# A recurrent two-layer kernel with streamed weights: half-size weight tiles, a deeper ring, later weight copies, and one-lane first and last steps

## The chip, the core and the metric

The kernel runs on one core of one Trainium2 chip. The metric is the device time of one execution in microseconds (us), the median of several. PE is the matrix engine, DVE the vector engine, ACT the scalar engine, POOL is GpSimd, SP the engine that here only issues DMAs. All timed runs of this study were in the fast state (mean granted PE clock of the profiled ones 0.981 to 0.992 of full speed).

## The reference

Two layers, A (attention with a memory that is carried from segment to segment) and B (dilated sliding-window attention), are applied twice: A, B, A, B.

```python
# A: S = 2048 tokens, Dm = 640, H = 32 heads of Dh = 192, segments of 32 tokens, memory of 8 tokens
mem = mem0
for s in range(64):
    h = concat([mem, x[32*s : 32*(s+1)]])         # 40 tokens
    q, k, v = h @ Wq, h @ Wk, h @ Wv              # 640 x 6144 each
    p = softmax(mask(q @ k.T * Dh**-0.5))
    o = (p @ v) @ Wo                              # 6144 x 640
    mem, out[s] = o[:8], o[8:]
# B: heads of 20, each token looks at itself and 7 tokens at distances 2, 4, ... 14
x = x + A(layernorm(x));  x = x + B(layernorm(x))
x = x + A(layernorm(x));  x = x + B(layernorm(x))
```

The memory makes the 64 segments sequential. Only part of the weights of A (31.5 MB) is kept on the chip; the rest is read again in every step.

## The kernel before

The second A, B pair runs three segments behind the first as a second *lane*: each step t handles segment t of the first pair and segment t - 3 of the second, 40 + 40 = 80 columns. So there are 67 steps. In the first three and the last three, one lane has nothing to do but is computed all the same. Eight groups of four heads make a step:

```python
def unit(self, kind, i):                       # one of 32 weight tiles of 983 KB
    ...
    if res: t_ = self.wres.tile([P, 3840], BF16, ...)          # 14 stay on the chip
    else:   t_ = self.wring.tile([P, 3840], BF16, name="w_ring")   # 18 pass through 4 slots
    if (kind, i) in self.wcopy:
        nc.sync.dma_start(out=t_[:], in_=self.wcopy[(kind, i)][:])    # rows of 7680 bytes
    else:
        nc.sync.dma_start(out=v, in_=src)                             # rows of 1536 or 1280 bytes
    ...
    elif (kind, i) not in self.wcopy:                                 # in step 0
        self.wcopy[(kind, i)] = self.dram.tile([P, 3840], BF16, ...)
        nc.gpsimd.dma_start(out=self.wcopy[(kind, i)][:], in_=t_[:])

def step(self, t):
    for i in range(NQUAD):                     # 8 groups
        self.a_k(i, t)                         # 30 matmuls of 80 columns, ACT copies the result
        self.a_q(i, t)                         # 30 of 80, DVE copies
        if i >= 2: self.a_o(i - 2)             # 30 of 80, into ps_acc
        if last: self.a_pv(i - 1); self.a_s(i)
        self.a_v(i, t)                         # 10 of 384
        if i >= 1 and not last: self.a_pv(i - 1)
        # ... here parts of layer B of the last two steps ...
        if not last: self.a_s(i)               # scores, 8 of 80
    # ... layer norm of the next segment, a_o(6), a_pv(7), B's projections, a_o(7), memory ...

def run(self, ctx):
    self.prologue()
    for t in range(self.n_seg + LAG + 2):      # the last two with layer B only
        self.step(t)
    self.y_store(yseg // 4)
```

The softmax here doesn't subtract the row's maximum and nothing guards it: scores larger than these inputs give would overflow.

Of the kernel before, what the change touches and what calls it, by code (L numbers as in the profile page):

```python
# [39 lines left out]
N_UNITS = 32  # L40
N_RES = 14
RING = 4


def unit_order():
    order = []
    for i in range(NQUAD):
        order.append(("k", i))
        order.append(("q", i))
        if i >= 2:  # L50
            order.append(("o", i - 2))
        order.append(("v", i))
    order += [("o", 6), ("o", 7)]
    return order


def resident_units():
    res = set()
    for n, u in enumerate(unit_order()):
        if (n * N_RES) // N_UNITS != ((n + 1) * N_RES) // N_UNITS:  # L60
            res.add(u)
    return res


class Kernel:
    def __init__(self, ctx, tc, A_x, A_mem0, A_Wq, A_Wk, A_Wv, A_Wo, B_wqkv, B_wo, out):
# [15 lines left out]
        self.ps_big = pool("ps_big", 4, space=PSUM)  # L82
# [4 lines left out]
        self.resident = resident_units()  # L87
        self.build_consts(B_wqkv, B_wo)

    def build_consts(self, B_wqkv, B_wo):  # L90
# [23 lines left out]

        def band(name, cur):
            m = cp.tile([P, NX], BF16, name=name)
            nc.gpsimd.memset(m[:], 0.0)
            for half in range(2):
                off = 0 if half == cur else SEG
                for l in range(2):  # L120
                    r0 = 64 * half + SEG * l
                    blk = m[r0:r0 + SEG, SEG * l:SEG * (l + 1)]
                    for w in range(BW):
                        nc.gpsimd.affine_select(out=blk, in_=blk, compare_op=ALU.not_equal, fill=1.0,
                                                base=off - BDIL * w, pattern=[[1, SEG]], channel_multiplier=-1)
            return m
# [19 lines left out]
        def pers(name, shape, n, dt=BF16, zero=True):  # L146
            ts = []
            for j in range(n):
                t_ = cp.tile(shape, dt, name=f"{name}{j}")
                if zero:  # L150
                    nc.vector.memset(t_[:], 0.0)
                ts.append(t_)
            return ts

        self.hT = pers("hT", [P, NC * NT + 88], 2)
        self.KF = pers("KF", [P, 4 * NT + 48], 2)
        self.Kz = pers("Kz", [P, 4 * NT + 48], 2)
        self.Vt = pers("Vt", [P, 1152], 2)
        self.xin = pers("xin", [P, NC, NX], 3)
        self.h2T = pers("h2T", [P, NC, P], 1)[0]  # L160
        self.KB = pers("KB", [P, NBC, P], 1)[0]
        self.VB = pers("VB", [P, BH // 2, 2 * BD + 1], 1)[0]
        nc.vector.memset(self.VB[:, :, BD:BD + 1], 1.0)
        self.On = pers("On", [P, 3 * P], 1)[0]
        self.YT = pers("YT", [P, NC, P], 1, zero=False)[0]
        self.m0T = pers("m0T", [P, NC, NM], 1, zero=False)[0]
        self.wqkv = cp.tile([P, NC, 3 * D], BF16, name="wqkv_sb")
        nc.scalar.dma_start(out=self.wqkv[:], in_=B_wqkv.rearrange("(c p) n -> p c n", p=P))
        self.wo = cp.tile([P, 2, 3, D], BF16, name="wo_sb")
        nc.vector.memset(self.wo[64:P, :, 2, :], 0.0)  # L170
        for par in range(2):
            r0 = par * (D // 2)
            nc.scalar.dma_start(out=self.wo[:, par, 0:2, :], in_=B_wo[r0:r0 + 2 * P, :].rearrange("(m p) n -> p m n", p=P))
            nc.scalar.dma_start(out=self.wo[0:64, par, 2, :], in_=B_wo[r0 + 2 * P:r0 + D // 2, :])

    def unit(self, kind, i):
        if (kind, i) in self.units:
            return self.units[(kind, i)]
        nc = self.nc
        res = (kind, i) in self.resident  # L180
        if kind == "o":
            src = self.wsrc["o"][QE * i:QE * (i + 1), :].rearrange("(m p) d -> p m d", p=P)
        else:
            src = self.wsrc[kind][:, QE * i:QE * (i + 1)].rearrange("(c p) n -> p c n", p=P)
        if res:
            t_ = self.wres.tile([P, 3840], BF16, name=f"w_{kind}{i}")
        else:
            t_ = self.wring.tile([P, 3840], BF16, name="w_ring")
        v = t_[:].rearrange("p (a b) -> p a b", a=6 if kind == "o" else NC)
        if (kind, i) in self.wcopy:  # L190
            nc.sync.dma_start(out=t_[:], in_=self.wcopy[(kind, i)][:])
        else:
            nc.sync.dma_start(out=v, in_=src)
        if res:
            self.units[(kind, i)] = v
        elif (kind, i) not in self.wcopy:
            self.wcopy[(kind, i)] = self.dram.tile([P, 3840], BF16, name=f"wc_{kind}{i}")
            nc.gpsimd.dma_start(out=self.wcopy[(kind, i)][:], in_=t_[:])
        return v
# [7 lines left out]
    def proj_stationary(self, kind, i, t):  # L207
        nc = self.nc
        w = self.unit(kind, i)
        hT = self.hT[t % 2]  # L210
        ps = self.big(f"ps_{kind}")
        for n in range(6):
            for c in range(NC):
                nc.tensor.matmul(ps[:, NT * n:NT * (n + 1)], lhsT=w[:, c, P * n:P * (n + 1)], rhs=hT[:, NT * c:NT * (c + 1)],  # L214
                                 start=(c == 0), stop=(c == NC - 1))
        return ps

    def a_k(self, i, t):
        nc = self.nc
        ps = self.proj_stationary("k", i, t)  # L220
        pv = ps[:, 0:6 * NT].rearrange("p (a b n) -> p a b n", a=2, b=3)
        h4 = lambda tl: tl[:, 0:4 * NT].rearrange("p (a j n) -> p a j n", a=2, j=2)
        kf, kz = h4(self.KF[i % 2]), h4(self.Kz[i % 2])
        nc.scalar.copy(out=kf, in_=pv[:, :, 0:3:2, :])  # L224
        nc.scalar.copy(out=kz[0:64, :, 0, :], in_=pv[0:64, :, 1, :])
        nc.scalar.copy(out=kz[64:P, :, 1, :], in_=pv[64:P, :, 1, :])

    def a_q(self, i, t):
        ps = self.proj_stationary("q", i, t)
        qt = self.ap2.tile([P, 6, NT], BF16, name="QT")  # L230
        self.nc.vector.tensor_copy(out=qt[:], in_=ps[:, 0:6 * NT].rearrange("p (a n) -> p a n", a=6))  # L231
        self.qt = qt

    def a_v(self, i, t):
        nc = self.nc
        w = self.unit("v", i)
        hT = self.hT[t % 2]
        vt = self.Vt[i % 2]
        for pr in range(2):
            ps = self.big("ps_v")  # L240
            for c in range(NC):
                nc.tensor.matmul(ps[:, 0:384], lhsT=hT[:, NT * c:NT * c + P], rhs=w[:, c, 384 * pr:384 * (pr + 1)],  # L242
                                 start=(c == 0), stop=(c == NC - 1))
            src = ps[0:NT, 0:384].rearrange("p (j e) -> p j e", j=2)
            dst = vt[0:NT, 512 * pr:512 * pr + 640].rearrange("p (j e) -> p j e", j=2)[:, :, 0:DH]
# [5 lines left out]
    def a_s(self, i):  # L251
        nc = self.nc
        ps = self.one("s")
        sv = ps[:, 0:4 * NT].rearrange("p (h n) -> p h n", h=4)
        kf, kz, qt = self.KF[i % 2], self.Kz[i % 2], self.qt
        for h in range(4):
            pr, j = h // 2, h % 2
            nc.tensor.matmul(sv[:, h, :], lhsT=kf[:, NT * h:NT * h + P], rhs=qt[:, 3 * pr + 2 * j, :], start=True, stop=False)  # L258
            nc.tensor.matmul(sv[:, h, :], lhsT=kz[:, NT * h:NT * h + P], rhs=qt[:, 3 * pr + 1, :], start=False, stop=True)  # L259
        e = self.ap2.tile([P, 4, NT], BF16, name="E")  # L260
        nc.scalar.activation(out=e[0:NT], in_=sv[0:NT], func=ACT.Exp, scale=float(DH) ** -0.5)  # L261
        em = self.ap2.tile([P, 4, NT], BF16, name="Em")
        nc.vector.tensor_tensor(out=em[0:NT], in0=e[0:NT], in1=self.maskA[0:NT, :].unsqueeze(1).to_broadcast([NT, 4, NT]), op=ALU.mult)
        self.em = em

    def a_pv(self, i):
        nc = self.nc
        em = self.em
        vt = self.Vt[i % 2]
        dn = self.one("d")  # L270
# [6 lines left out]
        r = self.ap2.tile([P, 2, 2, NT], F32, name="R")  # L277
# [9 lines left out]
    def a_o(self, i):  # L287
        nc = self.nc
        w = self.unit("o", i)
        ot = self.ots.pop(i)[:].rearrange("p a b n -> p (a b) n")  # L290
        if i == 0:
            self.acc = self.one("acc")
        for m in range(6):
            for c in range(NC):
                nc.tensor.matmul(self.acc[:, NT * c:NT * (c + 1)], lhsT=w[:, m, P * c:P * (c + 1)], rhs=ot[:, m, :],  # L295
# [5 lines left out]
    def mem_out(self, t):  # L301
        nc = self.nc
        a = self.lanes(self.acc[:, 0:NC * NT])
        h = self.lanes(self.hT[(t + 1) % 2][:, 0:NC * NT])
        if t + 1 == LAG:
            nc.vector.tensor_copy(out=h[:, :, 0, 0:NM], in_=a[:, :, 0, 0:NM])
            nc.vector.tensor_copy(out=h[:, :, 1, 0:NM], in_=self.m0T[:])
        else:
            nc.vector.tensor_copy(out=h[:, :, :, 0:NM], in_=a[:, :, :, 0:NM])

    def ln_sq(self, x):
        sq = self.bp.tile([P, NC, NX], BF16, name="sq")
# [11 lines left out]
    def ln_small(self, ps):  # L324
        nc = self.nc
        m = self.ap2.tile([P, NX], F32, name="ln_m")
# [3 lines left out]
        nc.vector.scalar_tensor_tensor(out=v[:], in0=ps[:, NX:2 * NX], scalar=1.0 / D, in1=v[:], op0=ALU.mult, op1=ALU.subtract)  # L330
        nc.scalar.activation(out=v[:], in_=v[:], func=ACT.Ln, bias=self.eps_t[:])
        r = self.ap2.tile([P, NX], F32, name="ln_r")
# [3 lines left out]
    def ln_big(self, x, mr, dst):  # L336
        nc = self.nc
        m, r = mr
        xc = self.bp.tile([P, NC, NX], F32, name="ln_xc")
# [5 lines left out]
    def b_x1(self, b):  # L345
        nc = self.nc
        a = self.lanes(self.acc[:, 0:NC * NT])
        x1 = self.x1p.tile([P, NC, NX], BF16, name="x1")
# [307 lines left out]
```

## Time and profile before

| | before |
|---|---|
| time, median of the four runs at hand for the prediction | 3563.71 us |
| span of the profiled run | 3561.9 us |
| PE busy | 97% of the span |
| weights read in a step | 17.7 MB |
| median step of steps 11 to 63, unhindered step | 51.25 us, 50.55 us |

The share of PE says little by itself: a run of 30 matmuls of 80 columns is recorded as 1.24 us, yet the next run starts 1.075 us after its start. The recorded end lies some 0.17 us late, so PE counts as busy in any gap shorter than that. What counts is the distance from start to start. The prediction below does that, stretch by stretch.

### The profile page before, as it was taken

How to read it: one execution, taken by the hardware profiler on the slowest of the kernel's cores; microseconds unless marked ns; L12 is line 12 of the kernel's file. 1: busy time of each engine (PE TensorE's matmuls, PEld its weight loads, DVE VectorE, ACT ScalarE, POOL GpSimd, SP SyncE). 2: the span in 40 equal slices, each digit the busy share in tenths (PEclk: the TensorE clock that was granted, in tenths of full speed). 3: DMA queues.
4: the chain of work that ended last, by engine and by line, in shares of the span. 5: the costliest groups of instructions: out<-in, count | busy, mean ns of one | idle time of the engine just before them, and what ended most of it. 6: DMA issues, size and time to landing. Idle time of an engine off the chain costs nothing.

```text
span 3561.9 us, 160052 instructions
## 1 busy us (share of the span) xinstructions
PE 3443.7 (97%) x72592; PEld 3003.7 (84%) x72592; DVE 2064.6 (58%) x5778; ACT 1676.0 (47%) x4723; POOL 67.3 (2%) x201
## 2 busy tenths in 40 slices
PE   4799999999999999999999999999999999999997
PEld 3688888888888888888888888888888888888886
DVE  2355655566555656665565665555655566656564
ACT  1244444445444444444445444445444444444443
POOL 2000000000000000000000000000000000000000
PEclk8799999999999999999999999999999999999998
DMA  9999999999999999999999999999999999999894
GB/s 380 396 351 348 361 347 345 346 366 348 345 344 360 340 341 352 356 345 346 351 351 346 353 358 342 340 347 362 349 343 346 356 348 346 355 352 346 336 364 169
DMA packets 199290, 1235.86 MB, mean 347 GB/s; under 512 B 20424, under 2 KB 42576, under 8 KB 198608
## 3 DMA queue, kind: packets, MB, share of 16 engines
q1 hardware_dynamic: 193088, 1199.39, 89.6%
q0 software_dynamic: 4160, 22.95, 1.6%
q8 instruction: 568, 9.31, 1.0%
q10 hardware_dynamic: 1360, 3.28, 0.2%
q14 instruction: 114, 0.93, 0.1%
HBM read 1205.22 MB, written 20.32 MB: 344 GB/s over the span
## 4 chain that ended last, share of the span: by engine, by line
PE 89%; DMA 6%; issue 4%; POOL 0%; SPq 0%; ACT 0%; DVE 0%; POOLq 0%; ACTq 0%
PE ps_v L242 23%; PE ps_k L214 15%; PE ps_acc L295 15%; PE ps_q L214 15%; PE ps_o L276 4%; DMA w_ring<-wc_v 3%; PE ps_bv L387 2%; PE ps_s L258 2%; PE ps_s L259 2%; PE ps_d L271 2%; PE ps_bq L367 2%; PE ps_bk L367 2%; PE ps_by L456 2%; PE ps_bs L411 1%; PE ps_st L321 1%
## 5 line engine op out<-in xcount | busy, mean ns | idle before, releaser
L249 ACT CAST Vt<-ps_v 80x384 bf16<-80x384 f32 x536 | 254.2, 474 | 1280.5 <-PE ps_v L242 1280.5
L242 PEld LDWEIGHTS <-hT 128*128 128x128 bf16 x5360 | 494.1, 99 | 302.1 <-issue 10.5
L282 DVE TENSOR_TENSOR OT<-ps_o,R 128x320 bf16<-128x320 f32 x536 | 263.6, 492 | 778.5 <-ACT R L280 771.6
L214 PEld LDWEIGHTS <-w_ring 128*128 128x128 bf16 x18090 | 687.5, 100 | 19.6 <-DMA w_ring<-in_A_Wq_dram 7.6
L242 PE MATMUL ps_v<-w_v,hT 128*128 128x384 bf16 x3350 | 605.4, 328 | 9.7 <-DMA w_v<-in_A_Wv_dram 8.3
L295 PE MATMUL ps_acc<-OT,w_ring 128*128 128x80 bf16 x12060 | 504.1, 203 | 19.4 <-DMA w_ring<-in_A_Wo_dram 11.4
L231 DVE CAST QT<-ps_q 128x480 bf16<-128x480 f32 x536 | 352.6, 658 | 232.6 <-PE ps_q L214 224.1
L295 PEld LDWEIGHTS <-w_ring 128*128 128x128 bf16 x12060 | 460.8, 100 | 22.0 <-DMA w_ring<-in_A_Wo_dram 12.2
L247 DVE CAST Vt<-ps_v 80x384 bf16<-80x384 f32 x536 | 296.3, 553 | 245.2 <-PE ps_v L242 236.8
L214 PE MATMUL ps_k<-hT,w_ring 128*128 128x80 bf16 x10050 | 418.9, 203 | 7.1 <-DMA w_ring<-in_A_Wk_dram 2.4
L242 PE MATMUL ps_v<-w_ring,hT 128*128 128x384 bf16 x2010 | 363.3, 328 | 7.0 <-DMA w_ring<-wc_v 3.8
L214 PE MATMUL ps_q<-hT,w_ring 128*128 128x80 bf16 x8040 | 335.4, 202 | 10.4 <-DMA w_ring<-in_A_Wq_dram 7.2
L214 PE MATMUL ps_q<-hT,w_q 128*128 128x80 bf16 x8040 | 333.8, 202 | 3.6 <-DMA w_q<-in_A_Wq_dram 3.2
L214 PEld LDWEIGHTS <-w_q 128*128 128x128 bf16 x8040 | 306.2, 100 | 4.1 <-DMA w_q<-in_A_Wq_dram 3.7
L224 ACT CAST KF<-ps_k 128x320 bf16<-128x320 f32 x536 | 226.9, 423 | 137.6 <-PE ps_k L214 137.6
L279 ACT ACTIVATE R<-ps_d 128x320 f32<-128x320 f32 x536 | 231.9, 433 | 106.4 <-PE ps_d L271 106.4
L276 PEld LDWEIGHTS <-Vt 80*128 80x128 bf16 x4288 | 221.4, 99 | 52.3 <-issue 4.4
L280 ACT ACTIVATE R<-R 128x320 f32<-128x320 f32 x536 | 251.9, 470 | 17.0
L214 PE MATMUL ps_k<-hT,w_k 128*128 128x80 bf16 x6030 | 250.4, 202 | 0.7 <-issue 0.5
L276 PE MATMUL ps_o<-Em,Vt 80*128 80x80 bf16 x4288 | 242.1, 200 | 3.1 <-issue 3.1
L261 ACT ACTIVATE E<-ps_s 80x320 bf16<-80x320 f32 x536 | 227.3, 424 | 24.3 <-PE ps_s L259 24.1
L214 PEld LDWEIGHTS <-w_k 128*128 128x128 bf16 x6030 | 229.4, 100 | 1.4 <-issue 1.0
(110 smaller groups left out, 4333.6 us busy)
## 6 DMA issues: line engine op xcount, KB each, us to landing
w_ring<-wc_o SPq DMA_DIRECT2D x396, 960.0 KB, 7.3
w_ring<-wc_k SPq DMA_DIRECT2D x330, 960.0 KB, 7.3
w_ring<-wc_q SPq DMA_DIRECT2D x264, 960.0 KB, 7.1
w_ring<-wc_v SPq DMA_DIRECT2D x198, 960.0 KB, 7.0
w_ring<-in_A_Wo_dram SPq DMA_DIRECT2D x6, 960.0 KB, 17.2
wc_o<-w_ring POOLq DMA_DIRECT2D x6, 960.0 KB, 8.3
w_ring<-in_A_Wk_dram SPq DMA_DIRECT2D x5, 960.0 KB, 16.8
w_v<-in_A_Wv_dram SPq DMA_DIRECT2D x5, 960.0 KB, 15.7
```

Of the source, the lines that this page charges most:

```text
L214: nc.tensor.matmul(ps[:, NT * n:NT * (n + 1)], lhsT=w[:, c, P * n:P * (n + 1)], rhs=hT[:, NT * c:NT * (c + 1)], start=(c == 0), stop=(c == ...
L224: nc.scalar.copy(out=kf, in_=pv[:, :, 0:3:2, :])
L231: self.nc.vector.tensor_copy(out=qt[:], in_=ps[:, 0:6 * NT].rearrange("p (a n) -> p a n", a=6))
L242: nc.tensor.matmul(ps[:, 0:384], lhsT=hT[:, NT * c:NT * c + P], rhs=w[:, c, 384 * pr:384 * (pr + 1)], start=(c == 0), stop=(c == NC - 1))
L247: nc.vector.tensor_copy(out=dst, in_=src)
L249: nc.scalar.copy(out=dst, in_=src)
L261: nc.scalar.activation(out=e[0:NT], in_=sv[0:NT], func=ACT.Exp, scale=float(DH) ** -0.5)
L276: nc.tensor.matmul(ov[:, pr, b, :], lhsT=vt[0:NT, 512 * pr + w0:512 * pr + w0 + P], rhs=em[0:NT, 2 * pr + j, :], start=st, stop=sp)
L279: nc.scalar.activation(out=rf, in_=dn[:, 0:4 * NT], func=ACT.Ln)
L280: nc.scalar.activation(out=rf, in_=rf, func=ACT.Exp, scale=-1.0)
L282: nc.vector.tensor_tensor(out=ot[:, :, 0:3:2, :], in0=ov[:, :, 0:3:2, :], in1=r[:], op=ALU.mult)
L295: nc.tensor.matmul(self.acc[:, NT * c:NT * (c + 1)], lhsT=w[:, m, P * c:P * (c + 1)], rhs=ot[:, m, :], start=(i == 0 and m == 0 and c == 0 ...
```

## The change

Its intent: less weight traffic, the same work in fewer matmuls, no idle lane, an earlier start, a shorter tail. The weight tiles are halved, 33 of 64 halves are resident, 31 pass through a ring of six half slots, spread evenly over PE's time. To find room for it, many double buffers become single ones, and two PSUM tiles (where matmuls accumulate) become one. The diff, cut to its core:

```diff
-N_UNITS = 32
-N_RES = 14
-RING = 4
+N_HALVES = 64
+N_PLACES = 39
+RING = 6
+COPY_STEPS = 10
...
+        self.streamed = {k: 1 + j % COPY_STEPS for j, k in enumerate(streamed_halves())}
+        self.x_load(0, self.nc.sync)                # first of all, ahead of the weights
...
+    def half(self, kind, i, h):
+        if key not in self.streamed:
+            t_ = self.wres.tile([P, 1920], BF16, name=f"w_{kind}{i}_{h}")
+            nc.sync.dma_start(out=view(t_), in_=src)           # k, q, v: rows of 768 bytes
...
+        t_ = self.wring.tile([P, 1920], BF16, name="w_ring")
+        if key in self.wcopy:
+            nc.sync.dma_start(out=t_[:], in_=self.wcopy[key][:])   # rows of 3840 bytes
         else:
+            nc.sync.dma_start(out=view(t_), in_=src)
+            if self.t == self.streamed[key]:        # about three copies a step, steps 1 to 10
+                self.wcopy[key] = self.dram.tile([P, 1920], BF16, ...)
+                nc.scalar.dma_start(out=view(self.wcopy[key]), in_=src)   # DRAM to DRAM
+
+    def active(self, t):                            # columns of the lanes that have work
+        l0, l1 = (0 if t < self.n_seg else 1), (2 if t >= LAG else 1)
+        return slice(LT * l0, LT * l1), slice(l0, l1)
...
-    a_k: ACT copies k three times; a_q: DVE copies q once
+    a_k: DVE copies k once;        a_q: ACT copies q three times (QF, Qz)
-    a_s: 8 score matmuls of 80 columns
+    a_s: 2 of 160 and 4 of 80;  a_pv puts the denominators into the same PSUM tile
-    b_wo: 30 matmuls of 64 columns
+    b_wo: 25 (the two half-filled weight blocks are joined)
...
         for i in range(NQUAD):
+            self.a_v(i, t)
+            if i >= 1: self.a_s(i - 1)              # scores one group later
+            self.a_k(i, t)
+            if last: self.a_pv(i - 1)
+            self.a_q(i, t)
+            if i >= 2: self.a_o(i - 2, t)
+            if last: self.a_s(i)
+            ...
+            elif i >= 1: self.a_pv(i - 1)
...
     def run(self, ctx):
         self.prologue()
+        self.build_b_consts(*self.wB)               # layer B's masks and weights afterwards, by POOL
-            for t in range(self.n_seg + LAG + 2):
+            for t in range(T):                      # T = 67
                 self.step(t)
+            self.drain(T - 2)                       # last two blocks of layer B, interleaved
```

## The prediction

> **What bounds the kernel now.** The program runs 67 recurrent steps (64 segments, and 3 more because the second layer pair runs three segments behind the first as a second "lane"), then a tail. I cut the span at the ends of the groups of 240 matmuls into ps_acc that close each step, and read busy time by stretch first: step 0, step 1, step 2, steps 3 to 10, 11 to 63, 64 to 66, the tail.
>
> ```profile
> core 0: us, PE busy (x) PEld busy (x) DVE busy (x) ACT busy (x) POOL busy (x), PEclk, DMA share, GB/s
> 0.00:139.68 139.68, 72.20 (x966) 56.65 (x966) 30.34 (x84) 23.78 (x62) 29.18 (x110) 0.79 1.03 385
> 139.68:191.74 52.06, 49.05 (x1002) 42.80 (x1003) 25.57 (x65) 22.05 (x62) 0.39 (x1) 0.97 1.00 396
> 191.74:242.30 50.56, 50.56 (x1087) 44.33 (x1084) 30.43 (x85) 24.67 (x70) 0.00 (x0) 1.00 0.93 354
> 242.30:651.52 409.22, 407.49 (x8670) 356.04 (x8666) 245.29 (x687) 199.17 (x563) 4.73 (x11) 1.00 0.93 350
> 651.52:3373.01 2721.49, 2696.30 (x57429) 2359.37 (x57426) 1629.27 (x4558) 1323.23 (x3736) 31.88 (x77) 1.00 0.93 349
> 3373.01:3525.09 152.08, 151.87 (x3245) 133.06 (x3241) 89.97 (x250) 74.19 (x209) 0.54 (x1) 1.00 0.87 328
> 3525.09:3561.95 36.86, 16.25 (x226) 11.50 (x221) 13.77 (x49) 8.93 (x21) 0.54 (x1) 0.68 0.02 5
> ```
>
> Step 0 is bound by the DMA: its share is 1.03 and PE is busy half the time. Afterwards PE is busy all the time, with the DMA just below full (0.93). DVE and ACT have room. The timeline of PE in a step shows that the matmuls stand back to back:
>
> ```profile
> 1037.06 0.57 PE L432 MATMUL ps_bo<-VB,EB 128*128 128x41 bf16 x16
> ...
> 1044.56 1.24 PE L214 MATMUL ps_q<-hT,w_ring 128*128 128x80 bf16 x30
> 1045.63 1.24 PE L295 MATMUL ps_acc<-OT,w_ring 128*128 128x80 bf16 x30
> 1046.71 1.79 PE L242 MATMUL ps_v<-w_v,hT 128*128 128x384 bf16 x10
> 1048.34 0.30 PE L271 MATMUL ps_d<-Em,ones 80*128 80x320 bf16 x1
> 1048.48 0.45 PE L276 MATMUL ps_o<-Em,Vt 80*128 80x80 bf16 x8
> 1048.76 1.04 PE L456 MATMUL ps_by<-OTB,wo_sb 128*128 128x64 bf16 x30
> ```
>
> From start to start, 30 matmuls of 80 columns take 1.075 us (35.8 ns each), 10 of 384 columns 1.63 us (163 ns), 30 of 64 columns 0.88 us (29.3 ns). So a pair of weight load and matmul costs its columns, not the load. The unhindered step is 50.56 us (the shortest found, many times); with the transposes of x and y in two steps of four it averages 50.70. Steps 11 to 63 average 2721.49/53 = 51.35. Only 0.65 us a step is stall. The waits of PE in that stretch say of what:
>
> ```profile
> PE ps_acc L295 <- issue: 6.1, 13, 1.3
> PE ps_v L242 <- DMA w_ring<-wc_v: 3.5, 8, 1.0
> PE ps_o L276 <- issue: 3.1, 2, 2.2
> ```
>
> About half are halts in mid-group of about 1 us that name no releaser (I take them for late instruction fetches, since 9.3 MB of instructions pass over the same DMA rings), part are late ring loads, and 0.09 us a step is ps_acc waiting for OT. So less weight traffic alone can win little in the middle: PE columns set the pace there.
>
> **What the Trainium skill says.** "TensorE: Matmul & The Clock Gate", section "Back-to-back issue gap", gives N/2.4 + 2.5 ns for a warm isolated matmul: 35.8, 162.5 and 29.2 ns for 80, 384 and 64 columns, which the trace meets. The same page, under "Wait — 56ns, not 53.3ns?", gives a floor of about 25 ns however few the columns; the trace agrees, 16 matmuls of 41 columns (ps_bo above) take 0.41 us to the next group, 25.6 ns each and not 19.6. "DMA: Bandwidth & Descriptors", section "Why small descriptors are slow", puts a fixed cost on each packet; in the trace's packet records a packet of 7680 bytes lasts 291 ns, 3840 bytes 149, 1536 bytes 65 and 1280 bytes 56 (medians), so about 8 ns are fixed. "Perfetto Trace Analysis", section "DMA Instruction — HWDGE", says the descriptor generator is shared and locked while an issue uses it; this trace shows issues from SP of up to 8.6 us while the rings are full, but none from ACT held so in the middle of work.
>
> **The change part by part.**
>
> *Weights.* Before, 18 of 32 units of 983 KB stream in each step: 17.7 MB. After, 64 halves of 491.5 KB, 33 resident and 31 streamed: 15.2 MB, 14% less, spread evenly over PE's time, with six half slots. Six slots at 50.6/31 = 1.63 us apart leave some 8 us from a free slot to its need. The engines moved 17.7 MB at 0.93 share in 51.35 us, so full speed is about 370 GB/s and 15.2 MB need 41 us of 50.5.
>
> *Step 0.* Before it moved 53.8 MB, 17.7 of them copies of the streamed units back to DRAM. After: the weights once, 31.5 MB, and 3.3 MB for layer B. But k, q and v halves are rows of 768 bytes, by my fit 65 - 0.037 x 768 = 37 to 38 ns each. 30,720 of these at 38, 6,144 rows of 1280 at 57, and 8.5 us for B, over 16 engines: 73 + 21.9 + 8.5 = 103 us. Packets overlap (share 1.03 in this step), so 100 us, plus 5 for the start, landing and the last matmuls: 105 against 139.7, **-34 us**. The early load of x and the later masks only feed a PE that waits for weights anyway.
>
> *Steps 1 and 2.* Only one lane is active; the 720 matmuls of k, q and o fall from 80 to 40 columns. PE would need about 43 us, but here nearly all 31 halves still come as 768-byte rows (24 of k, q, v at 1.5 us, 7 of o at 1.4) plus 3 or 4 DRAM copies: 49 to 51 us of DMA. **0 us** against 102.6 for the two.
>
> *Steps 3 to 10.* DMA work falls from about 47 to 42 us, below PE. Three copies a step are issued by ACT and may hold it. I take +0.4 us a step: **+3 us**.
>
> *Steps 11 to 63.* PE work: the scores go from 8 matmuls of 80 columns (287 ns) to 2 of 160 (69 each) and 4 of 80: 282, -0.04 us for eight; output projection of B from 30 to 25 at 29.2, -0.15; one more transpose, +0.06. Sum -0.13. The OT wait of 0.09 goes, as the last o(7) now has b_v and o(6) ahead of it (2.4 us against R at 0.9 and OT at 1.1 after ps_d and the b_k copy). A new one of about 0.1 enters at the last head group: q's three ACT copies end 0.32 + 0.30 + 0.29 + 0.2 = 1.1 us after q's last issue, o(5) covers 1.07. So 50.7 - 0.13 = 50.6 with the transposes; with 0.2 of remaining stall 50.8 against 51.35, **-29 us** in 53 steps. The move of k's copies to DVE and q's to ACT exchanges equal work; the reused score bank for the denominators, the single R and QX buffers have over 1.5 us between release and next need.
>
> *Steps 64 to 66.* One lane again, copies made: PE 50.6 - 720 x (35.8 - 25.6) ns = 43.2; DMA 41.4. With 0.8 of stall 44 each against 152.1 in all, **-20 us**.
>
> *Tail.* Layer B of the last two blocks is interleaved, but the chain through the softmax of the last block, its output, the transpose and the final store (5.6 us) stays. Adding up the durations of the old tail in the new order gives about 34 against 36.9: **-3 us**.
>
> Sum: -34 + 0 + 3 - 29 - 20 - 3 = -83: **3480 us**, 2.3% faster.
>
> **The rivals.**
>
> (a) The 768-byte rows are worse than my fit. No packet of that size is in the trace. At 46 ns, step 0 takes 15 us longer and steps 1 to 5 become DMA-bound by some 6 each: about 3520. Against it: 1280 and 1536 bytes fit one line with 7680.
>
> (b) ACT's DRAM copies are held by SP's full queue. 640 rows a load and about five loads outstanding is what blocked SP in step 0 (the fourth issue took 7.6 us). If each of 31 copies halts ACT, and so PE, for 1.5 us, +45: about 3525. For it: the shared generator. Against: ACT is only 47% busy, and an issue waits for one of SP's loads, about 1.5 us, not for the whole queue.
>
> (c) The new order makes PE wait elsewhere: v first, scores one group later, tighter single buffers. Each 0.3 us a step is 20 us. I followed the last group and the step's end with the durations of the trace and found nothing over 0.1.
>
> (d) The stalls vanish wholly, and the fetches too: steps 11 to 63 at 50.6, steps 1 and 2 near 46: about 3455.
>
> **Range and chances.** (a) and (b) push up by 40 each and I give each one in six; (d) pushes down by 25. So 3446 to 3512 eight times in ten. The 2% line lies at 3492, only 12 us above my number: chances 0.68 faster, 0.30 within 2%, 0.02 slower.
>
> **What would show it.** Right: step 0 ends near 105 us with the DMA share at 1.0; steps 1 and 2 near 51; middle steps 50.7 to 50.9 with DMA share near 0.8; last three near 44; chain still PE. Packets of 768 bytes near 38 ns. Wrong: packets of 46 ns or more; long DMA issues on ACT in steps 1 to 10, with PE waiting for ACT results; recurrent PE waits for QF, Qz or OT near the last group of a step; a middle step still at 51.3, which would say that the stalls never came from the weight traffic.

## The result, and the profile after

| | before | after |
|---|---|---|
| median of all runs taken for the result | 3566.58 us (13 runs) | 3474.36 us (8 runs, 3471.67 to 3479.44) |
| ratio of the fast runs | | 0.9741 (0.9728 to 0.9753) |
| span of the profiled run | 3561.9 us | 3469.1 us |

A ratio compares the fast runs of the two kernels in the same rounds, on the same chip, so it is not quite the ratio of the medians. Batches ran on different chips: between batches, compare ratios rather than microseconds. The change is 2.6% faster; 3480 was forecast, 3446 to 3512 as the range.

The same stretches as in the prediction, for the changed kernel: step 0, step 1, step 2, steps 3 to 10, 11 to 63, 64 to 66, the tail. The first number after the window is its length; at the end of a line stand the granted clock of PE, the DMA's busy share and its rate.

```profile
0.00:108.60 108.60, 64.23 (x950) 44.74 (x950) 28.53 (x87) 22.20 (x62) 21.30 (x93) 0.72 1.06 330
108.60:160.71 52.11, 44.07 (x986) 35.19 (x987) 22.84 (x65) 20.70 (x62) 0.97 (x2) 0.97 1.08 347
160.71:210.59 49.88, 44.58 (x1068) 37.09 (x1065) 27.20 (x84) 23.86 (x73) 0.00 (x0) 1.00 1.06 351
210.59:619.14 408.55, 406.01 (x8509) 355.18 (x8506) 243.22 (x690) 208.95 (x587) 4.81 (x11) 1.00 0.97 330
619.14:3304.22 2685.08, 2685.01 (x56369) 2354.19 (x56366) 1610.57 (x4559) 1387.08 (x3895) 33.01 (x77) 1.00 0.89 306
3304.22:3439.61 135.39, 131.34 (x3184) 110.74 (x3181) 81.77 (x251) 71.74 (x218) 0.55 (x1) 1.00 0.90 327
3439.61:3469.14 29.53, 14.29 (x218) 10.41 (x214) 13.52 (x49) 9.23 (x27) 0.54 (x1) 0.76 0.02 7
```

Set against the lines of before, stretch by stretch:

| stretch | before, us | after, us | difference | forecast |
|---|---|---|---|---|
| step 0 | 139.7 | 108.6 | -31.1 | -34 |
| steps 1 and 2 | 102.6 | 102.0 | -0.6 | 0 |
| steps 3 to 10 | 409.2 | 408.6 | -0.7 | +3 |
| steps 11 to 63 | 2721.5 | 2685.1 | -36.4 | -29 |
| steps 64 to 66 | 152.1 | 135.4 | -16.7 | -20 |
| tail | 36.9 | 29.5 | -7.3 | -3 |
| sum | 3561.9 | 3469.1 | -92.8 | -83 |

In the 53 middle steps of this run PE now halts nowhere for longer than its matmuls' recorded ends can hide: the list of PE's waits for this stretch, which named 6.1, 3.5 and 3.1 us in its first lines before, is empty. The steps take 50.5 or 50.8 us in turn (the transposes of x and y fall in every other step), one exception of 51.06 apart.

A look at the last head group of such a step shows what is left. Columns: start, recorded time, engine, line, operation, operands, count.

```profile
1015.66 0.70 PE L246 MATMUL ps_k<-hT,w_k 128*128 128x80 bf16 x15
1016.26 0.30 PE L306 MATMUL ps_s<-E,ones 80*128 80x320 bf16 x1
1016.40 0.45 PE L311 MATMUL ps_o<-E,Vt 80*128 80x80 bf16 x8
1016.68 0.70 PE L246 MATMUL ps_q<-hT,w_q 128*128 128x80 bf16 x15
1017.22 0.70 PE L246 MATMUL ps_q<-hT,w_ring 128*128 128x80 bf16 x15
1017.76 0.70 PE L332 MATMUL ps_acc<-OT,w_o 128*128 128x80 bf16 x15
1018.29 0.70 PE L332 MATMUL ps_acc<-OT,w_ring 128*128 128x80 bf16 x15
1018.92 0.23 PE L291 MATMUL ps_s<-Qz,KF 128*128 128x160 bf16 x1
```

A run of 15 matmuls of 80 columns takes 0.537 us. The last ps_acc run started at 1018.29, so the scores could have started at 1018.83; they started at 1018.92. That is the wait for ACT's q copies that the prediction expected (about 0.1 us, measured 0.09). In the same way the value product of group 6 (ps_s<-E,ones) could have started at 1016.20 and started at 1016.26: its masked exponentials were not ready, a wait that the prediction did not see. Both recur in each of the 53 steps (0.08 and 0.06 us in the median).

### The profile page after: what moved, and what is told of

It is laid out like the page before. It is cut to its first block, busy times and chain, and to the rows that moved or that the text cites. A ratio compares the mean times of both kernels' runs of the same rounds, so it can differ in the third digit from the quotient of the medians.

```text
span 3469.1 us, 158827 instructions
## 1 busy us (share of the span) xinstructions
PE 3389.5 (98%) x71252; PEld 2947.6 (85%) x71252; DVE 2027.6 (58%) x5781; ACT 1743.8 (50%) x4924; POOL 61.2 (2%) x185
## 3 DMA queue, kind: packets, MB, share of 16 engines
q14 instruction: 128, 1.05, 0.1%
## 4 chain that ended last, share of the span: by engine, by line
PE 92%; DMA 4%; issue 3%; SPq 0%; ACT 0%; DVE 0%; POOLq 0%; POOL 0%; DVEq 0%
PE ps_v L276 24%; PE ps_acc L332 16%; PE ps_q L246 15%; PE ps_k L246 15%; PE ps_o L311 4%; PE ps_bv L431 2%; DMA w_ring<-in_A_Wv_dram 2%; PE ps_s L291 2%; PE ps_s L306 2%; PE ps_s L296 2%; PE ps_bk L411 2%; PE ps_bs L455 2%; PE ps_bq L411 2%; PE ps_by L502 1%; PE ps_st L359 1%
## 5 line engine op out<-in xcount | busy, mean ns | idle before, releaser
L276 PE MATMUL ps_v<-w_ring,hT 128*128 128x384 bf16 x3685 | 695.2, 328 | 19.4 <-DMA w_ring<-in_A_Wv_dram 15.4
L246 PEld LDWEIGHTS <-w_ring 128*128 128x128 bf16 x13065 | 517.3, 100 | 21.0 <-DMA w_ring<-in_A_Wq_dram 7.5
L246 PE MATMUL ps_k<-hT,w_k 128*128 128x80 bf16 (+1 forms) x10050 | 440.2, 200 | 4.0 <-DMA w_k<-in_A_Wk_dram 3.0
L255 DVE CAST KF<-ps_k 128x480 bf16<-128x480 f32 (+1 forms) x536 | 337.5, 630 | 132.0 <-PE ps_k L246 131.9
L246 PE MATMUL ps_q<-hT,w_q 128*128 128x80 bf16 (+1 forms) x9045 | 405.6, 200 | 8.3 <-DMA w_q<-in_A_Wq_dram 6.9
L332 PE MATMUL ps_acc<-OT,w_o 128*128 128x80 bf16 (+1 forms) x9045 | 395.1, 200 | 7.5 <-DMA w_o<-in_A_Wo_dram 5.1
L332 PEld LDWEIGHTS <-w_o 128*128 128x128 bf16 x9045 | 347.1, 100 | 8.9 <-DMA w_o<-in_A_Wo_dram 5.9
L246 PE MATMUL ps_q<-hT,w_ring 128*128 128x80 bf16 (+1 forms) x7035 | 323.7, 200 | 8.4 <-DMA w_ring<-in_A_Wq_dram 6.4
L332 PE MATMUL ps_acc<-OT,w_ring 128*128 128x80 bf16 (+1 forms) x7035 | 324.1, 200 | 4.4 <-DMA w_ring<-in_A_Wo_dram 4.2
L332 PEld LDWEIGHTS <-w_ring 128*128 128x128 bf16 x7035 | 280.6, 100 | 10.7 <-DMA w_ring<-in_A_Wo_dram 5.0
L246 PE MATMUL ps_k<-hT,w_ring 128*128 128x80 bf16 (+1 forms) x6030 | 277.5, 200 | 2.9 <-issue 1.7
```

The source lines that it names most:

```text
L246: nc.tensor.matmul(pv[:, n, cs], lhsT=w[:, c, P * (n % 3):P * (n % 3 + 1)], rhs=hT[:, c, cs], start=(c == 0), stop=(c == NC - 1))
L255: self.nc.vector.tensor_copy(out=self.lanes_cols(self.KF[i % 2], 6)[:, :, cs], in_=self.lanes_cols(ps, 6)[:, :, cs])
L276: nc.tensor.matmul(ps[:, 0:384], lhsT=hT[:, NT * c:NT * c + P], rhs=w[:, c, :], start=(c == 0), stop=(c == NC - 1))
L332: nc.tensor.matmul(av[:, c, cs], lhsT=w[:, m % 3, P * c:P * (c + 1)], rhs=ot[:, m, cs], start=(i == 0 and m == 0 and c == 0), stop=(i == N ...
```

## The experiments

My theory after the result: three things make the gain. Step 0 is shorter because its DMA bytes are fewer. The middle steps lose their stalls because the weight traffic fell. The last three are shorter because PE has half the columns. The rivals: the new order or the finer ring took the stalls away, not the traffic; the copies and their engine matter elsewhere than thought.

Twelve runs were made, all of them the changed kernel with one edit, except where said. The edits are cut to their core. Step times are from the profiled execution of each run, cut as above.

**The old traffic in the new kernel.**

```diff
-N_PLACES = 39
+N_PLACES = 34
```

> The changed kernel with five more halves streamed instead of resident: 36 of 64, that is 17.7 MB a step as in the kernel before, with the new order, halves and ring kept. Theory T (the stalls of the middle steps came from the weight traffic, both as late loads and as halts inside a group of matmuls): steps 11 to 63 go from 50.66 us back to 51.1 to 51.4 with a DMA share of 0.93 and halts of about 1 us in mid-group; with longer early steps (more 768-byte rows) and last steps near 48 us the total is about 3530. Rival R (the new order or the finer ring took the stalls away, not the traffic): the middle steps stay at 50.7 to 50.8 and the total stays under 3510.

Measured: 3536.13 us (ratio 0.9896, 0.9872 to 0.992), middle steps 50.96 us, DMA share 0.96, steps 1 and 2 at 58.3 and 57.2, steps 3 to 10 at 53.6, the last three at 47.4. The total went where the theory put it, but more by the first ten steps (34 us) than by the middle ones (16 us), which came out between theory and rival. PE's waits in the middle stretch, the first four (us in total, times, longest; "issue" stands where the profile shows nothing that released PE):

```profile
PE ps_v L276 <- DMA w_ring<-wc_v: 2.2, 5, 1.0
PE ps_acc L332 <- DMA w_ring<-wc_o: 1.9, 4, 0.9
PE ps_k L246 <- DMA w_ring<-wc_k: 1.5, 3, 0.8
PE ps_bq L411 <- issue: 1.2, 3, 0.7
```

Late ring loads are back, but the halts that name no releaser add up to 2.2 us in this list (1.2 here, two more entries of 0.6 and 0.4), against 16.5 in the kernel before with the same bytes a step. So the same bytes cost 0.30 us a step over the changed kernel here, while the old structure stood 0.65 above its unhindered step. Late loads need not come from the bytes as such: 36 halves in six slots also follow each other faster than 31 (see the shorter ring below).

**Less traffic in the old kernel.** The kernel before, with two streamed units replaced by resident ones. This computes with wrong weights on purpose (the comparison with the reference let it pass all the same).

```diff
 # the kernel before
     def unit(self, kind, i):
+        kind, i = {("v", 4): ("v", 3), ("o", 4): ("o", 3)}.get((kind, i), (kind, i))
```

> The kernel before, with two of its 18 streamed units replaced by units that are already resident (wrong result on purpose): 15.7 MB a step, everything else as it was, old order included. Theory T: the middle steps fall from 51.35 to 50.75 to 50.9 us; step 0, bound by the DMA, loses two loads and two copies, about 10 us; total 3515 to 3525. Rival R: the middle steps stay at 51.2 or more and only step 0 is shorter: about 3555.

Measured: 3521.68 us (ratio 0.9855), middle steps 50.79 us, step 0 128.6 us. The theory's numbers hold on every count. (The ratio has the interval 0.9834 to 0.9876, so the difference is clear of noise.) The line of the middle stretch:

```profile
638.23:3330.18 2691.95, 2688.51 (x57430) 2357.47 (x57426) 1627.84 (x4558) 1322.47 (x3736) 31.89 (x77) 1.00 0.86 314
```

With 15.7 MB a step the old order and the old ring of whole units are within 0.1 us of their unhindered average of 50.70. Two streamed units less would have brought 0.56 of the 0.69 us; the new structure alone 0.39 (51.35 to 50.96). The two overlap: each removes the same stalls, and with both none are left. Two things are not separated by this: 16 units in four slots, not 18, also leave each slot more time, and "the new structure" is order, halves and ring together.

**A shorter ring.** The same 33 resident halves, the same traffic, four slots instead of six.

```diff
-N_PLACES = 39
-RING = 6
+N_PLACES = 37
+RING = 4
```

> The changed kernel with four half slots in the ring instead of six, the same 33 resident halves and the same traffic. Theory: four slots leave about 5 us from a free slot to its need, against 4.7 to 5.2 us from issue to landing, so late loads return: middle steps of 51 to 53 us, total +20 to +120. Rival (average traffic alone decides): middle steps stay under 50.8, total within +5.

Measured: 3667.49 us (ratio 1.0265), 2.7% slower than the kernel before; middle steps 53.07 us at a DMA share of only 0.87. PE's waits in the middle stretch, its first two lines:

```profile
PE ps_v L276 <- DMA w_ring<-wc_v: 37.0, 78, 2.0
PE ps_q L246 <- DMA w_ring<-wc_q: 22.3, 44, 1.3
```

At 50.6/31 = 1.63 us from one streamed half to the next, four slots are 6.5 us, less the time that PE itself uses a slot, and a load takes 4.8 to 5.0 us from issue to landing in this run. Six slots are 9.8 us. So the reserve in the ring, not the average load of the DMA, decides about late loads. The same estimate for all kernels here (slots times spacing at the unhindered step, less the median time from issue to landing, less PE's own use of about 0.6 us for a half and 1.2 for a unit) gives 1.0 us for this run, 2.0 with the old traffic, 2.9 for the kernel before, 3.5 without copies (next run), 4.3 for the changed kernel and 4.7 for the two aliases. PE's waits for ring loads in the 53 steps are, in this order, 78.6, 6.0, 4.9, 0, 0 and 0 us.

**No copies at all.** The streamed halves come as short rows of the inputs in every step.

```diff
-            if self.t == self.streamed[key]:
+            if self.t < 0:
```

> The changed kernel with no copies to DRAM at all: the 31 streamed halves are read as 768- and 1280-byte rows of the inputs in every step. By the packet times of the changed kernel's trace (36 to 41 ns for 768 bytes, 55 to 60 for 1280, 149 to 177 for 3840) a step needs 44 to 48 us of the DMA instead of 38 to 43, still below PE's 50.5. Theory: DMA share near 0.93 and middle steps of 50.8 to 51.1, steps 1 and 2 some 2 us shorter without the copies, steps 64 to 66 near 47 to 49; total +10 to +30, about 3495. Rival (rows of 768 bytes are as good as copies once the ring has its lead): middle steps stay at 50.66, only steps 64 to 66 grow; total within +10.

Measured: 3476.04 us (ratio 0.9744). The rival was right: steps 11 to 63 in one line, then 64 to 66:

```profile
612.94:3301.07 2688.13, 2685.45 (x56369) 2353.95 (x56366) 1609.92 (x4559) 1389.07 (x3895) 32.95 (x77) 1.00 0.97 305
3301.07:3444.63 143.56, 134.55 (x3184) 111.77 (x3181) 81.89 (x251) 72.08 (x218) 0.55 (x1) 0.99 1.00 309
```

The DMA is busy 0.97 of the time, more than in the kernel before with its 0.93, and yet the middle steps stay at 50.72 us: no ring load is late, and only three halts without a named releaser (2.0, 0.3 and 0.3 us) are lost. Steps 1 and 2 fall to 50.2 and 47.7 us and steps 3 to 10 to 50.67, without the copies' traffic; the last three, where PE needs only 43 us, take 47.9 us a step at a DMA share of 1.00 (PE's list there has 1.8 us of late ring loads and 6.1 us of halts without a named releaser). What the copies win at the end, they cost at the beginning: as made here, they win nothing.

**All copies in step 0**, as before the change (there from the ring slot, here from DRAM to DRAM).

```diff
-        self.streamed = {k: 1 + j % COPY_STEPS for ...}
+        self.streamed = {k: 0 for ...}
```

> The changed kernel with all 31 copies made in step 0 instead of three a step in steps 1 to 10. Theory (step 0 is bound by the DMA, so its bytes count one for one): 15.2 MB more at the 330 GB/s of that step make it 40 to 46 us longer, 150 us; steps 1 and 2 fall to 44 to 46 us each, steps 3 to 10 to 50.7; total +25 to +30, about 3503. Rival (the copies hide beside the waits for weights): step 0 grows by under 20 us and the total falls.

Measured: 3491.22 us (ratio 0.9786). Step 0 grew by 29.8 us to 138.4 (DMA share 1.06, 363 GB/s), less than the 40 to 46 of the theory. It moved 50.2 MB where the changed kernel moves 35.8, so 14.4 MB more in 29.8 us. The DMA share is the same, but a packet of 768 bytes took 36 ns in the median of this step, not 40. Steps 1 and 2 fell to 46.3 and 44.2, steps 3 to 10 to 50.68. The direction is the theory's: step 0 pays for its bytes, and deferring them makes nearly all of its gain, of which later steps give back about half. One thing here bears on rival (b): two of ACT's issues took 7.1 and 2.4 us (at 23.3 and 30.7 us), the first while an issue of SP, begun at 20.7 us, took 10.3. So an issue on ACT can be held; the other 29 took 0.55 to 0.84 us.

**The copies issued by POOL instead of ACT.**

```diff
-                nc.scalar.dma_start(out=view(self.wcopy[key]), in_=src)
+                nc.gpsimd.dma_start(out=view(self.wcopy[key]), in_=src)
```

> The changed kernel with the copies issued by GpSimd instead of ACT. Theory: an issue on ACT takes 0.55 us and holds nothing on PE's path, so steps 1 to 10 and the total stay within 4 us (3470 to 3478). Rival (b) of the prediction (ACT is held by its DMA issues): steps 3 to 10 fall from 51.07 to 50.7 us, total -3 to -10.

Measured: 3508.39 us (ratio 0.9835), 34 us slower. Neither theory had that. Step 0 took 118.0 us and steps 3 to 10 54.4 each. POOL's timeline in step 3:

```profile
236.46 0.53 POOL L530 COPY xin<-XT 128x160 bf16<-128x160 bf16 x1 [114.21 <-ACT XT L525]
236.94 1.63 POOL L224 DMA_DIRECT2D wc_v<-in_A_Wv_dram  x2
238.23 1.08 POOL L224 DMA_DIRECT2D wc_o<-in_A_Wo_dram  x1
238.81 0.82 POOL L530 COPY xin<-XT 128x160 bf16<-128x160 bf16 x1
239.07 1.37 POOL L224 DMA_DIRECT2D wc_q<-in_A_Wq_dram  x1
239.72 1.56 POOL L224 DMA_DIRECT2D wc_k<-in_A_Wk_dram  x1
240.36 1.74 POOL L224 DMA_DIRECT2D wc_v<-in_A_Wv_dram  x1
```

These copies wait for nothing in the program. POOL has little else to do, so it runs ahead until an x copy stops it (for 114 us here), then issues the copies of two steps, six, within 4 us: 2.9 MB that push in between the ring's loads. About 10 us later PE waits for v's half, the first line of its waits in steps 3 to 10:

```profile
PE ps_v L276 <- DMA w_ring<-in_A_Wv_dram: 18.8, 7, 5.1
```

On ACT the same copies stand between ACT's other work and go out 16.5 us apart in the median (125.4, 142.0, 158.5, 163.3, 177.9 us and so on), 0.55 to 0.66 us each. So rival (b) of the prediction, ACT held by its DMA issues, did not come in the changed kernel, and ACT's ordinary work is the throttle that keeps the copies apart. That the burst delays the ring is read from the times; I made no run with POOL's copies spaced out, and POOL's copies also pass through another DMA queue (q0, software_dynamic, where ACT's are in q10, hardware_dynamic), which is left as a rival.

**Both lanes always.**

```diff
-        l0, l1 = (0 if t < self.n_seg else 1), (2 if t >= LAG else 1)
+        l0, l1 = 0, 2
```

> The changed kernel with both lanes always computed, 80 columns in all steps. Theory: steps 64 to 66 go from 45.1 us back to 50.6 (+16 us), steps 1 and 2 stay within 1 us each because the DMA sets their length, step 0 stays; total about 3491. Rival (PE counts in the first steps too): steps 1 and 2 also gain 3 us or more each, total about 3497 or more.

Measured: 3489.03 us (ratio 0.9766 against 0.9741, so 9 us more by the ratios; by the medians, of different chips, 15). Steps 64 to 66 take 151.7 us against 135.4, steps 1 and 2 51.6 and 50.8 against 52.1 and 49.9. The theory holds in the steps: the idle lane is worth 10 to 17 us at the end (the last three took 134.8 to 141.9 us in the eight profiled executions that do the same work there), and nothing at the beginning, where the DMA share is 1.06 to 1.08 without the idle lane and 1.04 to 1.07 with it.

**The old serial tail.**

```diff
     def drain(self, b):
-        # blocks b and b + 1 interleaved
+        # all of b: scores, value product, transpose, output; then v, k, q and all of b + 1
```

> The changed kernel with the tail in the old serial order (block 65 to its end, then block 66). Theory: the tail goes from 29.5 to about 36.5 us, total +7, about 3481, nothing else moves. Rival (the shorter tail comes from other things than the interleaving, such as five projections matmuls less and a warm clock): under +3 us.

Measured: 3479.62 us (ratio 0.974), tail 35.7 us against 29.5. The theory holds in the profile, +6.2 us in the tail. The totals, from different chips, differ by 5 us, the ratios (0.974 and 0.9741) not at all, so the total does not show it.

**The old beginning**, in a batch with the unaltered changed kernel on the same chip.

```diff
-        self.x_load(0, self.nc.sync)          # in the constructor, and m0 likewise
+        self.x_load(0)                        # by GpSimd, in the prologue
-        self.prologue(); self.build_b_consts(*self.wB)   # B's loads by gpsimd
+        self.build_b_consts(*self.wB); self.prologue()   # B's loads by scalar
```

> The changed kernel unaltered, on the chip of the three other runs, as their yardstick: ratio to the kernel before 0.972 to 0.976.

> The changed kernel with the old beginning: layer B's weights issued by ACT at once, layer B's masks built before the first load of x, x loaded and the first segment copied by GpSimd. Theory (step 0 waits for weights whatever PE does early): PE starts about 20 us later, yet step 0 ends within 2 us of the unaltered kernel's, total within 3 us. Rival (PE's late start is carried to the end of step 0): +8 us or more.

Measured: unaltered 3474.15 us (ratio 0.9728), old beginning 3479.39 (0.9746). The yardstick came as expected; both expectations of the beginning missed (+5.2 us in all). PE's first matmul comes at 26.1 us instead of 5.3, and step 0 ends at 113.9 us instead of 109.2:

```profile
0.00:113.87 113.87, 61.31 (x950) 44.06 (x950) 28.50 (x86) 22.17 (x62) 19.18 (x91) 0.79 1.01 314
```

The DMA share of step 0 is 1.01, with 314 GB/s, where the unaltered kernel has 1.05 and 329 for the same bytes: with PE late, ring slots come free late, and loads are issued late: the 21st weight load goes out at 43.1 us instead of 38.2, the 61st at 101.5 instead of 96.6. So about 5 of the 21 us by which PE starts earlier reach the end of step 0.

**Another order in the last head group**, to take away the two waits shown above, same batch.

```diff
             if last:
-                self.a_k(i, t); self.a_pv(i - 1); self.a_q(i, t)
+                self.a_q(i, t); self.a_k(i, t); self.a_pv(i - 1)
```

> The changed kernel with the last head group of each step in the order q, k, then the value product of group 6, where the changed kernel has k, value product, q. In its trace that group costs two waits a step: 0.086 us before the scores of group 7 (ACT's three q copies outlast the output projection) and 0.075 us before the value product of group 6 (its mask is not ready). Theory: both vanish, middle steps fall from 50.66 to 50.50 us, total -9 to -11 us, ratio lower by 0.0025 to 0.003. Rival (the waits only move, to the copies of k on DVE or to the score bank): under -3 us.

Measured: 3470.92 us (ratio 0.9719, 0.9699 to 0.9738). The mechanism is confirmed, the gain is not. Both waits are gone:

```profile
1019.33 0.70 PE L246 MATMUL ps_k<-hT,w_ring 128*128 128x80 bf16 x15
1019.87 0.70 PE L246 MATMUL ps_k<-hT,w_k 128*128 128x80 bf16 x15
1020.40 0.30 PE L306 MATMUL ps_s<-E,ones 80*128 80x320 bf16 x1
1020.55 0.45 PE L311 MATMUL ps_o<-E,Vt 80*128 80x80 bf16 x8
1020.83 0.71 PE L332 MATMUL ps_acc<-OT,w_o 128*128 128x80 bf16 x15
1021.37 0.70 PE L332 MATMUL ps_acc<-OT,w_ring 128*128 128x80 bf16 x15
1021.91 0.23 PE L291 MATMUL ps_s<-Qz,KF 128*128 128x160 bf16 x1
```

From 1019.87 to 1020.40 and from 1021.37 to 1021.91 are 0.53 and 0.54 us, a run of 15 matmuls without a gap. The shortest step fell from 50.51 to 50.38 us, but single halts without a named releaser (2.5 us before ps_acc in all, the longest 1.6) leave the mean at 50.61 against 50.69 of the yardstick in this batch. The total is 3.2 us lower and the intervals overlap: not shown to be faster.

**The same order, and the copies one a step in steps 3 to 33.**

```diff
+        # the order of the previous run
-        self.streamed = {k: 1 + j % COPY_STEPS for ...}
+        self.streamed = {k: 3 + j for ...}
```

> The order of the previous run, and the DRAM copies begun in step 3 and made one a step (steps 3 to 33) instead of three a step in steps 1 to 10. Theory: besides the order's -10, steps 1 and 2 fall by 2 us each as in the run without copies, steps 3 to 10 by 0.3 each, and steps 64 to 66 keep their 45 us: total -15 to -18 against the changed kernel, ratio near 0.969. Rival (each copy costs the same whenever it is made): no better than the order alone.

Measured: 3471.78 us (ratio 0.9717, 0.9697 to 0.9737). In the profiled execution, the fastest of its four (3463.84), the early steps fell as expected: 50.0 and 47.4 us for steps 1 and 2, 50.66 for steps 3 to 10. The other three took 3471.6 to 3472.5. Its ratio cannot be told from that of the order alone or of the yardstick. A version that surely beats the changed kernel was not found.

## Why the prediction was right

The time lay 6 us below the forecast. Step 0, the middle steps and the last three make the gain, as forecast, but the middle steps give the most and not step 0. By its steps:

- *"Step 0 is bound by the DMA"*, 105 us: right, 108.6. The term mis-sized is the packet: 768-byte rows took 40 ns and 1280-byte rows 60 in the median of step 0, not 38 and 57; and 35.8 MB passed in this time, not 34.8, because loads of step 1 begin in it. The share was 1.06, near the 1.03 used. That the early start "only feeds a PE that waits" was wrong by 5 us, as the old beginning showed. Rival (a), rows at 46 ns, did not come.
- *Steps 1 and 2*, 0: right (-0.6), for the reason given; with both lanes on they are as long.
- *Steps 3 to 10*, +3: measured -0.7. The copies cost what was taken, 0.4 us a step (51.07 against 50.67 without them). What the sum left out is that the stall of the old steps (51.15 on average) goes here too. The reason feared was not the one: ACT's issues held nothing; rival (b) did not come.
- *Steps 11 to 63*, -29: measured -36.4. The term that failed is "0.2 of remaining stall", which was 0. The work on PE fell by about 0.13 us as added up, the OT wait of 0.09 went, and two waits of 0.15 together came, one foreseen and one not; so the unhindered average moved only from 50.70 to 50.66. Nearly the whole gain here is the removed stall. That fewer streamed units take it away is shown by the old kernel with two aliases; that this is not alone, by the new kernel with the old traffic.
- *"I take them for late instruction fetches"*: the traces bear it out. The profile lists packets of 16 KB in a queue of their own (q8, "instruction": 9.3 MB, 64 bytes for each of PE's 145,184 recorded instructions), one every 6 us in the median. In the 14 traces PE halts 192 times without a named releaser in steps 1 to 66, and every one of these halts ends 1.21 to 1.61 us after such a packet has ended; of the 535 halts with a named releaser, 52 do. Why the fetches came late so often in the old structure is open: in the middle steps the halts fell from 16.5 us to 2.2 with the same bytes in the new structure, and to 2.5 in the old kernel with less traffic.
- *Steps 64 to 66*, -20: measured -16.7. The forecast PE time of 43.2 us is near the 44.1 us of the last of them; the other two took 45.4 and 45.9. The 0.8 us allowed for stall was too little, and the stall was not late weights: PE's list for the three names no DMA, but 3.0 us of the halts just described and 0.8 us of others. With both lanes on, where a matmul lasts 35.8 ns and not 25.3, the same list is empty.
- *Tail*, -3: measured -7.3. Adding up durations in a row missed that block b's value product and output stand beside block b + 1's scores; the serial tail costs 6.2 us more.
- *Rival (c)*, waits from the new order: 0.15 us a step, half of the 0.3 set there as an example. *Rival (d)* came true in its first half (no stalls at all in the profiled run), not in its second (steps 1 and 2 at 46).

In part the closeness is luck: two of the six terms promised too much, by 6.2 us together (step 0, the last three), and four too little, by 16.0, so the sum is off by 9.8 us and not by 22. The total is off by only 6, because the profiled run was 3.5 us faster than the median.

## What to carry to other kernels

Where the pace is set by the matrix engine's columns and the DMA runs close beside it, a cut in traffic bought only the stalls: find the unhindered step first, and the mean minus that is all there is to win. Look at the reserve of the ring (slots times spacing, less own use, against issue to landing) and not at the DMA's busy share: 0.97 with six slots made no load late, 0.87 with four cost 2.4 us a step. A DMA that waits for nothing goes out when its engine gets to it, so the engine that issues background copies is also their throttle (so it looks in the POOL run; its rival is said there). And halts that name no releaser can be set against the packets of the instruction queue: here all of them fit.

## What the Trainium skill lacked or had wrong

- "TensorE: Matmul & The Clock Gate", section "Back-to-back issue gap", says that in a stream of weight loads and matmuls both set the spacing, about 81 ns at 128 columns. Here each matmul has its own weight load (57,429 and 57,426 recorded in the middle steps before) and the spacing is that of the matmul alone: 35.8 ns at 80 columns, 163 ns at 384, and four of 128 columns in 0.23 us, 57 ns each. The page's formula for the isolated matmul fits; its figure for the stream does not. Its floor of about 25 ns holds with a weight load each: 15 matmuls of 40 columns in 0.38 us, 25.3 ns each.
- "DMA: Bandwidth & Descriptors", section "Why small descriptors are slow", gives a fixed cost per packet but no duration by size. The packet medians here are 36 ns for 768 bytes (40 in step 0), 55 for 1280, 149 for 3840 and 291 for 7680.
- "Perfetto Trace Analysis", section "DMA Instruction — HWDGE", describes the lock on the descriptor generator, but not how long it holds another engine. In the changed kernel it held nothing (all 31 issues on ACT took 0.55 to 0.66 us while SP's queue was loaded); with all copies in step 0, an issue on ACT took 7.1 us beside one on SP of 10.3.
- No page says that the choice of the issuing engine spaces the transfers: the same 31 copies cost 34 us more from POOL, which issued six within 4 us, than from ACT, which issued them 16.5 us apart in the median.
- No page gives the delay from the end of an instruction packet to PE's restart: 1.21 to 1.61 us in all 192 halts.
